# A chunked delta-rule attention in front of two gated MLPs: whole-row stages, four quarter-array matmuls at a time, and one pool of five PSUM banks

## The chip, the cores and the metric

The kernel runs on one core of a Trainium2 chip. The metric is the device time of one execution in microseconds. The core has a matmul engine (PE), which writes to eight PSUM banks, a vector engine (DVE), an activation engine (ACT), a general engine (POOL) and a queue that issues DMAs (SP). Each of them works through its own list of instructions in order, and they wait for one another with semaphores.

## The reference

Four batches of eight heads, a sequence of 768 and a head size of 48. For every head a 48 by 48 state is carried along the sequence. The result goes through two MLPs over 3072 tokens.

```python
k_n = k / (np.linalg.norm(k, axis=-1, keepdims=True) + 1e-06)
for t in range(S):
    kt, vt, bt = (k_n[:, :, t], v[:, :, t], beta[:, :, t, None])
    y[:, :, t] = np.einsum('bhd,bhde->bhe', q[:, :, t], state)
    v_old = np.einsum('bhde,bhd->bhe', state, kt)
    state = state + bt[:, :, :, None] * np.einsum('bhd,bhe->bhde', kt, vt - v_old)
...
rms = np.sqrt(np.mean(x * x, axis=-1, keepdims=True) + 1e-06)
xn = x / rms * rms_g
g = xn @ w_gate
silu = g * (1.0 / (1.0 + np.exp(-g)))
x = silu * (xn @ w_val) @ w_out
...
h = x @ w_in
sp = np.where(h > 20.0, h, np.log1p(np.exp(np.minimum(h, 20.0))))
y = (h * np.tanh(sp)) @ w_out
```

## The kernel before

The sequence is cut into twelve rows of 64 steps. A row holds 32 heads: 16 pairs, a pair's two heads in the two halves of the 128 partitions. Within a row the recurrence becomes matmuls, and for that a triangular 64 by 64 system is inverted per head. One inversion serves a segment of two rows and runs mostly on DVE (`inlane`): it begins with `comp` (L488) and ends with the transposes into `X` and `yc` (L580, L584). Two small PE stages for each row then finish it (`merge32`, L601 and L611). The inversion of segment s+1 is worked on while the rows of segment s run.

A row `r` is a list of stages (`chain_row`). Its stages are, with the line of their main instruction:

- `turn_q`, `turn_k` (L480): transposes of q and k on PE; `norm`, `scale_k` (L407, L420, L430, L431): the norms of a later row's k; `products` and `scores` (`gram`, L465, L472): k times k for a later segment, k times q for this row. DVE takes both out of PSUM with a mask (L472, tile `A` or `PT`).
- `residual` (L778): state times k, subtracted from v by DVE (L784).
- `values` (L799): the inverse times that, copied by ACT into `ve` (L801).
- `outputs` (L817 for the state's part, L825 for the row's own): the result `po`, copied out by ACT (L832), scaled by DVE (`scale_x`, L873) and transposed for the MLP (`to_x`, L888).
- `kv_update` (L854): adds k times values to the state `sx` on DVE (L862).

Four of these stages are done in two halves (`r0 r1`, `v0 v1`, `o0 o1`, `k0 k1`), two batches in a half. The state `sx` is spread: a pair's two 48 by 48 states stand as a block diagonal over 128 partitions and 96 columns, so that one matmul of 128 rows and 96 columns serves two heads. Row 0 has no state to read and row 11 none to write.

Beside a row run the first third of the first MLP (`part_a`: `pg`, `pv`, `pd`, L201 to L203 and L218 to L220), the inversion, and at some rows the splitting of weights into a high and a low part (`convs`, L122 to L159). `merge` interleaves these streams by planned costs (`C`), so that each engine gets one fixed list. Row orders are written out by hand: `EVEN`, `ODD`, and `R0`, `R1` for the first two rows. After row 11 come the rest of the weights, the rest of the first MLP and the second one, all of it matmuls of 128 by 128.

The attention has five PSUM banks: two in `ps_c` for the four halved stages, three in `ps_p` for the rest.

Of the kernel before, what the change touches and what calls it, by code (L numbers as in the profile page):

```python
# [21 lines left out]
    EVEN="nA q0 r1 x1 q1 r0 p v0 o0 k0 v1 s0 o1 k1 nB s1 x0".split(),  # L22
    ODD="q0 nA r0 r1 q1 nB c0 x1 v0 v1 p o0 c1 s0 o1 k0 d0 g x0 d1 k1 h s1".split(),
    R0="x1 r1 r0 q0 q1 p nA v0 v1 o0 o1 s0 nB k0 s1 x0 k1".split(),
    R1="r0 nA q0 x1 q1 c0 p r1 v0 o0 c1 nB v1 o1 s1 g s0 d0 k0 d1 k1 x0 h".split(),
    PRE="n2 t00 t01 w1 g0 s1 w2 s2 n3 t10 | t11 c g1 c c s3 t20 c t21 | t30 g2 t31 w3 g3".split(),
    C=dict(n=0.263, q=0.454, r=0.262, p=1.6, v=1.308, o=1.237, k=1.065, s=0.184, x=0.323, c=0.14, d=0.231, g=2.2, h=1.6),
# [30 lines left out]
def kernel(  # L58
# [14 lines left out]
    nc = tc.nc  # L73
# [193 lines left out]
    def phase_b1():  # L267
# [14 lines left out]
        ps_c = st_a.enter_context(pool("ps_c", 2, space=PSUM))  # L282
        ps_p = st_a.enter_context(pool("ps_p", 4 - P["PSD"], space=PSUM))
# [25 lines left out]
        sx = [kp.tile([128, 2, 2, 2, 2, D], F32, name=f"sx{i}") for i in range(2)]  # L309

        kT_t, A_t, X11_t, v_t, x_t, nr_t = {}, {}, {}, {}, {}, {}

# [15 lines left out]
        def load_v(r):  # L328
            if r < NR:
                v_t[r] = rp.tile([128, 16, D], F32, tag="v", name="v")  # L330
                load(v_t[r], v, r)
# [4 lines left out]
        def setup():  # L336
            qsrc = beta[:, :, 0:2 * C].rearrange("b (j e) (r f h t) -> e f r (b j) h t", e=2, r=2, f=2, t=16)
            def load_bq(r):
                for g in range(4):
                    nc.sync.dma_start(out=bq[g * 32:g * 32 + 32, r], in_=qsrc[g // 2, g % 2, r])  # L340
# [20 lines left out]
            for t in vep + sx:  # L361
                nc.gpsimd.memset(t, 0.0)
# [28 lines left out]
            for e in range(2):  # L391
                for f in range(2):
                    for r in range(2):
                        p0 = e * 64 + f * 32 + r * 16
                        nc.sync.dma_start(out=bl[p0:p0 + 16], in_=bsrc[e, f, r])
# [41 lines left out]
        def turn_k(r, bp, ps=None):  # L437
# [5 lines left out]
            if r > 3:  # L443
                need(("p", r - 4), ("r", r - 4, 0), ("r", r - 4, 1))
# [3 lines left out]
        def products(r, soft=False):  # L448
# [3 lines left out]
            if rl == 0:  # L452
                need(*([("v", r - 3, 0), ("v", r - 3, 1)] if sg > 1 else []))
                A_t[sg] = As[sg % 2]
            need(("T", r, 0), ("T", r, 1))
            gram(("G", r), kT_t[r], kT_t[r], mneg, A_t[sg][:, rl * 16:rl * 16 + 16, :], soft)
            yield 1

        def gram(key, kT, xT, mask, dst, soft=False):

            pss = [ps_p.tile([128, 8, 64], F32, tag="pp", name="pp") for _ in range(2)]
            for i in range(8):
                for j, e in ((0, 0), (1, 1), (0, 1), (1, 0)):
                    rows, sl = slice(j * 64, (j + 1) * 64), slice(e * 64, (e + 1) * 64)
                    nc.tensor.matmul(pss[j][sl, i, :], kT[rows, i // 2, i % 2, sl], xT[rows, i // 2, i % 2, sl])  # L465
# [9 lines left out]
        def turn(nat, bp, dstT, key, ps=None):  # L475
            if ps is None:
                ps = ps_p.tile([128, 4, 128], F32, tag="pp", name="pp")
# [115 lines left out]
        def merge32(r, X11, Z):  # L593
# [3 lines left out]
            ps = ps_p.tile([128, 16, 32], F32, tag="pp", name="pp")  # L597
# [9 lines left out]
            ps = ps_p.tile([128, 16, 32], F32, tag="pp", name="pp")  # L607
# [99 lines left out]
        def quick_products(r):  # L707
# [4 lines left out]
            def small(lhsT, rhs, groups=(0, 32, 64, 96), ps=None):  # L712
                if ps is None:
                    ps = ps_p.tile([128, 16, 32], F32, tag="pp", name="pp")
# [39 lines left out]
        def chain_row(r):  # L754
# [14 lines left out]
            def residual(bp):  # L769
                done.add(("r", r, bp))  # L770
                if r == 0:
                    return
                need(("s", r, bp))
                ps = ps_c.tile([128, 8, D], F32, tag="c", name="c")
                for b in range(2):
                    for jj in range(2):
                        for e in range(2):
                            nc.tensor.matmul(  # L778
                                ps[e * 64:(e + 1) * 64, b * 4 + jj * 2:b * 4 + jj * 2 + 2, :],
                                kT[:, bp * 2 + b, jj, e * 64:(e + 1) * 64],  # L780
                                sx[bp][:, b, jj, e],
                            )
                R = vv[:, bp * 8:bp * 8 + 8, :]
                nc.vector.tensor_tensor(out=R, in0=R, in1=ps, op=ALU.subtract)  # L784
# [7 lines left out]
            def values(bp):  # L792
                ps = ps_c.tile([128, 8, D], F32, tag="c", name="c")
                need(("r", r, bp), ("Y", r))
                for i in range(8):
                    u = bp * 8 + i
                    for e in range(2):
                        o = e * 64
                        nc.tensor.matmul(ps[o:o + 64, i, :], Y[o:o + 64, rl * 16 + u, :], vv[o:o + 64, u, :])  # L799
                for e in range(2):  # L800
                    nc.scalar.copy(vep[bp][e * 64:(e + 1) * 64, :, e, :], ps[e * 64:(e + 1) * 64])  # L801
                if bp == 1:
                    need(("v", r, 0))
                done.add(("v", r, bp))
                if bp == 1:
                    load_v(r + 1)
                yield 1

            def outputs(bp):
                need(("v", r, bp), ("p", r), ("s", r, bp) if r else ("p", r))  # L810
                ps = ps_c.tile([128, 2, 2, 2, D], F32, tag="c", name="o")
                halves2 = [slice(b * 64, (b + 1) * 64) for b in range(2)]
                if r > 0:
# [428 lines left out]
```

## Time and profile before

| | us |
|---|---|
| median of 3 runs | 1229.4 (1228.05 to 1229.65) |
| the profiled execution | 1227.23 |
| span in its profile | 1225.3 |
| PE busy | 1132.1 (92%) |
| DVE busy | 751.1 (61%) |
| ACT busy | 507.6 (41%) |
| POOL busy | 536.5 (44%) |

Shares of the whole span say little here, because the attention stands only in the first 490 us or so. Times in the rows below are microseconds from the start of the span. A row of a timeline gives start, duration, engine, line, operation, tiles and shapes, the number of instructions it merges, and in brackets how long the engine was idle before it and what it waited for. A matmul in 32-bit floats leaves two records, so a stage of 32 matmuls shows as x64.

### The profile page before, as it was taken

How to read it: one execution, taken by the hardware profiler on the slowest of the kernel's cores; microseconds unless marked ns; L12 is line 12 of the kernel's file. 1: busy time of each engine (PE TensorE's matmuls, PEld its weight loads, DVE VectorE, ACT ScalarE, POOL GpSimd, SP SyncE). 2: the span in 40 equal slices, each digit the busy share in tenths (PEclk: the TensorE clock that was granted, in tenths of full speed). 3: DMA queues.
4: the chain of work that ended last, by engine and by line, in shares of the span. 5: the costliest groups of instructions: out<-in, count | busy, mean ns of one | idle time of the engine just before them, and what ended most of it. 6: DMA issues, size and time to landing. Idle time of an engine off the chain costs nothing.

```text
span 1225.3 us, 30099 instructions
## 1 busy us (share of the span) xinstructions
PE 1132.1 (92%) x13044; PEld 1093.0 (89%) x13044; DVE 751.1 (61%) x1155; ACT 507.6 (41%) x878; POOL 536.5 (44%) x442
## 2 busy tenths in 40 slices
PE   6675889899898987999999999988999999999998
PEld 6664779788797877999999999988999999999998
DVE  7999995869688699455555542368434433343333
ACT  3344435353434554212111111163757555555672
POOL 7466584747636365334434432244323232232232
PEclk9668989899899998999999999998999999999999
DMA  6133231323222645434333231421111101111101
GB/s 151 30 80 92 67 79 55 79 54 79 54 66 66 182 143 168 129 112 147 112 109 102 84 113 65 142 91 58 33 40 40 39 14 40 39 40 40 36 5 26
DMA packets 121044, 95.05 MB, mean 78 GB/s; under 512 B 80336, under 2 KB 103504, under 8 KB 120912
## 3 DMA queue, kind: packets, MB, share of 16 engines
q1 hardware_dynamic: 108816, 69.53, 20.4%
q10 hardware_dynamic: 12096, 23.60, 5.7%
q8 instruction: 102, 1.67, 0.6%
q14 instruction: 30, 0.25, 0.1%
HBM read 64.80 MB, written 28.31 MB: 76 GB/s over the span
## 4 chain that ended last, share of the span: by engine, by line
PE 64%; DVE 12%; issue 2%; POOL 1%; ACT 1%; DMA 0%; SPq 0%; POOLq 0%; DVEq 0%
PE pd L1138 5%; PE pd L1139 5%; PE pd L1137 5%; PE ph L202 5%; PE ph L201 5%; PE ph L203 5%; PE pv L201 3%; PE pd L218 3%; PE pd L219 3%; PE pd L220 3%; PE pv L202 3%; PE pv L203 3%; PE pg L201 3%; PE pg L203 3%; PE pg L202 3%; DVE t L142 2%
## 5 line engine op out<-in xcount | busy, mean ns | idle before, releaser
L1185 POOL TENSOR_TENSOR gl<-t,gh 128x512 fp32r<-128x512 f32 x96 | 125.2, 1305 | 254.6 <-DVE gh L1184 253.2
L246 POOL TENSOR_TENSOR hl<-sg,hh 128x512 fp32r<-128x512 f32 x72 | 106.6, 1481 | 172.7 <-DVE hh L245 165.0
L201 PE MATMUL ph<-xh,wih 128*128 128x256 f32 x576 | 162.8, 283 | 4.6 <-DVE t L1181 4.6
L202 PE MATMUL ph<-xl,wih 128*128 128x256 f32 x576 | 162.6, 282 | 0.0
L203 PE MATMUL ph<-xh,wil 128*128 128x256 f32 x576 | 162.5, 282 | 0.0
L236 ACT ACTIVATE sg<-pg 128x512 f32<-128x512 f32 x72 | 43.0, 597 | 229.5 <-PE pg L203 202.2
L218 PE MATMUL pd<-hh,woh 128*128 128x256 f32 x432 | 125.7, 291 | 11.1 <-ACT par L937 6.4
L1137 PE MATMUL pd<-wqh,gh 128*128 128x384 f32 x384 | 130.3, 339 | 1.9 <-DVE wqh L158 1.9
L1138 PE MATMUL pd<-wql,gh 128*128 128x384 f32 x384 | 130.3, 339 | 1.7 <-POOL wql L159 1.7
L1139 PE MATMUL pd<-wqh,gl 128*128 128x384 f32 x384 | 130.0, 338 | 0.0
L201 PE MATMUL pv<-xh,wvh 128*128 128x256 f32 x432 | 127.3, 295 | 0.0
L201 PE MATMUL pg<-xh,wgh 128*128 128x256 f32 x432 | 126.2, 292 | 0.0
L202 PE MATMUL pg<-xl,wgh 128*128 128x256 f32 x432 | 122.6, 284 | 3.9 <-POOL xl L894 3.6
L220 PE MATMUL pd<-hh,wol 128*128 128x256 f32 x432 | 122.3, 283 | 4.1 <-POOL wol L159 4.1
L219 PE MATMUL pd<-hl,woh 128*128 128x256 f32 x432 | 122.5, 284 | 1.0 <-POOL hl L246 1.0
L202 PE MATMUL pv<-xl,wvh 128*128 128x256 f32 x432 | 123.3, 285 | 0.0
L203 PE MATMUL pv<-xh,wvl 128*128 128x256 f32 x432 | 123.2, 285 | 0.0
L203 PE MATMUL pg<-xh,wgl 128*128 128x256 f32 x432 | 122.3, 283 | 0.0
L1181 DVE TENSOR_TENSOR t<-t,ph 128x512 f32<-128x512 f32 x96 | 65.2, 680 | 83.4 <-ACT t L1179 83.4
L242 DVE TENSOR_TENSOR sg<-sg,pv 128x512 f32<-128x512 f32 x72 | 49.4, 686 | 107.0 <-PE pv L203 104.2
L201 PEld LDWEIGHTS ph<-xh,wih 128*128 128x128 f32 x576 | 109.8, 191 | 4.8 <-DVE t L1181 4.8
L202 PEld LDWEIGHTS ph<-xl,wih 128*128 128x128 f32 x576 | 109.9, 191 | 0.0
(197 smaller groups left out, 3007.8 us busy)
## 6 DMA issues: line engine op xcount, KB each, us to landing
raw<-in_moe_w_out_dram SPq DMA_DIRECT2D x28, 384.0 KB, 3.7
raw<-in_moe_w_in_dram SPq DMA_DIRECT2D x16, 384.0 KB, 3.8
kh<-in_k_dram SPq DMA_DIRECT2D x24, 192.0 KB, 3.6
qp<-in_q_dram SPq DMA_DIRECT2D x24, 192.0 KB, 4.3
v<-in_v_dram SPq DMA_DIRECT2D x24, 192.0 KB, 3.9
raw<-in_moe_w_gate_dram SPq DMA_DIRECT2D x12, 384.0 KB, 4.0
raw<-in_moe_w_val_dram SPq DMA_DIRECT2D x12, 384.0 KB, 3.6
xh_d<-xh SPq DMA_DIRECT2D x12, 384.0 KB, 3.2
```

The lines of the kernel that those rows point to most:

```text
L201: nc.tensor.matmul(ps[:, f, :], wh[:, kt, sl], xh[:, kt, :], start=(kt == 0), stop=False)
L202: nc.tensor.matmul(ps[:, f, :], wh[:, kt, sl], xl[:, kt, :], start=False, stop=False)
L203: nc.tensor.matmul(ps[:, f, :], wl[:, kt, sl], xh[:, kt, :], start=False, stop=(kt == KD - 1))
L218: nc.tensor.matmul(ps, wh[:, f, sl], hh[:, f, :], start=(i + f == 0), stop=False)
L219: nc.tensor.matmul(ps, wh[:, f, sl], hl[:, f, :], start=False, stop=False)
L220: nc.tensor.matmul(ps, wl[:, f, sl], hh[:, f, :], start=False, stop=last)
L246: nc.gpsimd.tensor_tensor(out=hl, in0=sg, in1=hh.bitcast(F32), op=ALU.subtract)
L1137: nc.tensor.matmul(ps, gh[:, f, sl], wh[:, f, :], start=(m + f == 0), stop=False)
L1138: nc.tensor.matmul(ps, gh[:, f, sl], wl[:, f, :], start=False, stop=False)
L1139: nc.tensor.matmul(ps, gl[:, f, sl], wh[:, f, :], start=False, stop=last)
L1181: nc.vector.tensor_tensor(out=t, in0=t, in1=ps, op=ALU.mult)
L1185: nc.gpsimd.tensor_tensor(out=gl, in0=t, in1=gh.bitcast(F32), op=ALU.subtract)
```

## The change

`residual`, `values` and `kv_update` become one stage for the whole row, and the state's part of `outputs` becomes a stage of its own for the whole row (`of_state`, in the row lists `y`). The state is no longer spread: `sx` is one tile, and each head's 48 by 48 state is read by a matmul of 64 rows, 64 columns of weights and 48 streamed columns. These matmuls are issued so that four in a row lie in the four quarters of the array, and they write two banks. For that the two halves of the partitions are swapped for two of the batches, and so v, beta and the k products of those batches are laid out swapped; v is loaded by four DMAs in place of two, and beta by 16 and 16 in place of 8 and 8. `kv_update` stands ahead of the outputs, DVE adds the state in two instructions of 128 partitions in place of four of 48, and ACT copies `po` in two pieces. All five banks are in one pool. The row lists, `PRE` and the planned costs are new.

```diff
-    EVEN="nA q0 r1 x1 q1 r0 p v0 o0 k0 v1 s0 o1 k1 nB s1 x0".split(),
-    ODD="q0 nA r0 r1 q1 nB c0 x1 v0 v1 p o0 c1 s0 o1 k0 d0 g x0 d1 k1 h s1".split(),
+    EVEN="r nA q0 x1 q1 y p v k o0 nB o1 s0 s1 x0".split(),
+    ODD="r nA q0 q1 x1 y nB c0 p v c1 k o0 d0 o1 g s0 x0 d1 h s1".split(),
...
-    C=dict(n=0.263, q=0.454, r=0.262, p=1.6, v=1.308, o=1.237, k=1.065, s=0.184, x=0.323, c=0.14, d=0.231, g=2.2, h=1.6),
+    C=dict(n=0.263, q=0.454, r=0.8, y=0.8, p=1.6, v=1.6, o=1.0, k=1.2, s=0.184, x=0.323, c=0.3, d=0.3, g=1.6, h=1.6),
...
-        ps_c = st_a.enter_context(pool("ps_c", 2, space=PSUM))
-        ps_p = st_a.enter_context(pool("ps_p", 4 - P["PSD"], space=PSUM))
+        ps_a = st_a.enter_context(pool("ps_a", 6 - P["PSD"], space=PSUM))
...
             def load_bq(r):
                 for g in range(4):
-                    nc.sync.dma_start(out=bq[g * 32:g * 32 + 32, r], in_=qsrc[g // 2, g % 2, r])
+                    for bp in range(2):
+                        o = g * 32 + bp * 16
+                        nc.sync.dma_start(
+                            out=bq[o:o + 16, r], in_=qsrc[(g // 2) ^ bp, g % 2, r, bp * 8:bp * 8 + 8]
+                        )
...
+            def residual():
+                done.add(("r", r))
+                if r == 0:
+                    return
+                need(("s", r))
+                pss = [bank(8, D) for _ in range(2)]
+                for i, (b, jj) in enumerate(units()):
+                    for j, e in ((0, 0), (1, 1), (0, 1), (1, 0)):
+                        nc.tensor.matmul(
+                            pss[j][part(e ^ (b // 2)), i, :], kT[part(j), b, jj, part(e)], sx[part(j), b, jj, e]
+                        )
+                for j, ps in enumerate(pss):
+                    R = vv.rearrange("p (i j) d -> p j i d", j=2)[:, j]
+                    nc.vector.tensor_tensor(out=R, in0=R, in1=ps, op=ALU.subtract)
...
+            def values():
+                need(("r", r), ("Y", r))
+                pss = [bank(8, D) for _ in range(2)]
                 for i in range(8):
+                    for bp, o in ((0, 0), (1, 1), (0, 1), (1, 0)):
+                        u = bp * 8 + i
+                        nc.tensor.matmul(
+                            pss[bp][part(o ^ bp), i, :], Y[part(o), rl * 16 + u, :], vv[part(o), u, :]
+                        )
...
-                for j2 in range(2):
-                    o = j2 * 64
-                    d = sx[bp][o:o + D, :, :, :, j2, :].rearrange("p b j e d -> p (b j e) d")
...
+                for e, ps in enumerate(pss):
+                    d = sx[:, :, :, e, :].rearrange("p b j d -> p (b j) d")
+                    nc.vector.tensor_tensor(out=d, in0=d, in1=ps, op=ALU.add)
```

The first place is DVE's list at the turn from an odd row to an even one, where a new inversion begins. Before:

```order
L862 TENSOR_TENSOR sx_188<-sx_188,kv 48x8x48 x2
L472 TENSOR_TENSOR A_182<-pp,mneg 128x8x64 x2
L873 SCALAR_TENSOR_TENSOR po<-po,rv,gB 128x384
L407 TENSOR_REDUCE ss<-sq 128x16
L488 SCALAR_TENSOR_TENSOR comp<-A_182,h_165 128x1024
L784 TENSOR_TENSOR v<-v,c 128x384
L495 STREAM_TRANSPOSE N__170<-comp 128x1024
L784 TENSOR_TENSOR v<-v,c 128x384
```

With the change:

```order
L487 TENSOR_TENSOR A_179<-pp,mneg 128x8x64 x2
L893 SCALAR_TENSOR_TENSOR po<-po,rv,gB 128x384
L487 TENSOR_TENSOR A_179<-pp,mneg 128x8x64 x2
L893 SCALAR_TENSOR_TENSOR po<-po,rv,gB 128x384
L800 TENSOR_TENSOR v<-v,pp 128x8x48 x2
L503 SCALAR_TENSOR_TENSOR comp<-A_179,h_162 128x1024
L420 TENSOR_REDUCE ss<-sq 128x16
L510 STREAM_TRANSPOSE N__167<-comp 128x1024
```

The even row's two subtractions (`v`) now stand ahead of `comp` and the norm's sum (`ss`) behind it; the state's addition (`sx`) of the odd row has gone up, to behind `yc`.

The second place is DVE's list in the middle of an odd row, from the sum `ss` to the scores `PT`. Before:

```order
L407 TENSOR_REDUCE ss<-sq 128x16
L784 TENSOR_TENSOR v<-v,c 128x384
L570 TENSOR_REDUCE X__171<-pr 128x4x16
L784 TENSOR_TENSOR v<-v,c 128x384
L430 RECIPROCAL rn<-nr 128x16
```

With the change:

```order
L800 TENSOR_TENSOR v<-v,pp 128x8x48 x2
L529 TENSOR_TENSOR pr<-X__168,T_4664 128x1024
L420 TENSOR_REDUCE ss<-sq 128x16
L585 TENSOR_REDUCE X__168<-pr 128x4x16
L529 TENSOR_TENSOR pr<-X__168,T_4664 128x768
L585 TENSOR_REDUCE X__168<-pr 128x4x16
L443 RECIPROCAL rn<-nr 128x16
L588 TENSOR_REDUCE X__168<-prp 128x4x16
L487 TENSOR_TENSOR PT<-pp,mpos 128x8x64 x2
```

The reciprocal `rn`, which needs two POOL instructions on `ss`, now stands behind two sums and a product in place of one sum and two subtractions.

The third place is PE's list in the same odd row, without the rows of `part_a` between. Before:

```order
L799 MATMUL c<-v,A_183 64x48 x16
...
L465 MATMUL pp<-QT,kT_181 64x64 x32
...
L817 MATMUL o<-sx_188,QT 64x2x48 x8
L825 MATMUL o<-ve_186,PT 64x96 x8
...
L854 MATMUL kv<-ve_185,kh_175 48x96 x8
...
L480 MATMUL pp<-ident,kh_174 128x128 x4
L465 MATMUL pp<-kT_180 64x64 x32
L601 MATMUL pp<-X_4637,A_182 32x32 x32
```

With the change:

```order
L813 MATMUL pp<-sx,QT 64x48 x32
...
L478 MATMUL pp<-QT,kT_178 64x64 x32
...
L832 MATMUL pp<-v,A_180 64x48 x32
...
L881 MATMUL pp<-ve_182,kh_172 64x48 x16
L881 MATMUL pp<-ve_183,kh_172 64x48 x16
...
L848 MATMUL pp<-ve_183,PT 64x96 x8
L616 MATMUL pp<-X_4977,A_179 32x32 x32
L478 MATMUL pp<-kT_177 64x64 x32
```

The values (L832) now come behind the scores (L478), and the k products that stood ahead of the first `merge32` matmuls (L601, now L616) come behind them. When the values begin, the state's products hold two of the five banks and the scores two more.

## Rows read from the trace of the kernel before

**Rows 1.** Windows: PE, loads, DVE, ACT, POOL busy (counts), PE clock, DMA share, GB/s.

```profile
60.00:134.00 74.00, 53.10 (x1282) 46.53 (x1280) 72.31 (x105) 36.59 (x72) 43.01 (x34) 0.77 0.31 77
134.00:206.00 72.00, 63.77 (x1159) 57.80 (x1158) 55.98 (x79) 29.42 (x61) 44.96 (x31) 0.95 0.27 68
...
275.40:341.10 65.70, 58.99 (x1075) 53.53 (x1075) 52.58 (x74) 25.82 (x54) 41.43 (x29) 0.95 0.24 62
...
403.50:487.00 83.50, 69.81 (x884) 64.85 (x878) 76.01 (x122) 42.88 (x98) 44.36 (x42) 0.96 0.58 181
```

**Rows 2.** Timeline of DVE through one segment (rows 6 and 7).

```profile
274.50 0.95 DVE L407 TENSOR_REDUCE ss<-sq 128x16 f32<-128x768 f32 x1 [3.01 <-ACT sq L405]
275.37 1.27 DVE L488 SCALAR_TENSOR_TENSOR comp<-A,h 128x1024 f32<-128x1024 f32 x1
...
290.62 1.11 DVE L862 TENSOR_TENSOR sx<-sx,kv 48x384 f32<-48x384 f32 x2
...
310.24 1.21 DVE L570 TENSOR_REDUCE X__171<-pr 128x64 f32<-128x1024 f32 x1
...
314.20 0.25 DVE L430 RECIPROCAL rn<-nr 128x16 f32<-128x16 f32 x1 [2.28 <-POOL nr L421]
314.37 1.36 DVE L514 TENSOR_TENSOR pr<-X__171,T 128x768 f32<-128x768 f32 x1
...
319.97 1.28 DVE L472 TENSOR_TENSOR PT<-pp,mpos 128x512 f32<-128x512 f32 x2
...
323.26 1.92 DVE L584 STREAM_TRANSPOSE yc<-N__170 128x1024 f32<-128x1024 f32 x1
...
344.56 0.56 DVE L784 TENSOR_TENSOR v<-v,c 128x384 f32<-128x384 f32 x1 [2.21 <-PE c L778]
```

**Rows 3.** What DVE waited for from 134 to 403 us: total, times, longest.

```profile
DVE rn L430 <- POOL nr L421: 6.9, 3, 2.3
```

**Rows 4.** Timeline of PE through the same segment: its waits and the `merge32` stages.

```profile
271.19 1.20 PE L611 MATMUL pp<-A,N__170 32*32 32x32 f32 x64
...
299.33 0.55 PE L888 MATMUL pp<-ident,po 128*128 128x128 f32 x3 [1.86 <-DVE po L873]
...
310.38 1.95 PE L799 MATMUL c<-v,A 64*64 64x48 f32 x32 [3.44 <-DVE v L784]
...
327.65 0.28 PE L201 MATMUL pv<-xh,wvh 128*128 128x256 f32 x1
327.77 0.28 PE L202 MATMUL pv<-xl,wvh 128*128 128x256 f32 x1
...
329.98 1.20 PE L601 MATMUL pp<-X,A 32*32 32x32 f32 x64
...
340.85 1.20 PE L611 MATMUL pp<-A,N__170 32*32 32x32 f32 x64
```

**Rows 5.** Timeline of PE in row 4, at full clock: the halved stages and the scores.

```profile
204.56 0.88 PE L778 MATMUL c<-sx,kT 128*64 128x96 f32 x16
...
208.18 1.16 PE L465 MATMUL pp<-QT,kT 64*64 64x64 f32 x64
...
211.58 1.14 PE L799 MATMUL c<-v,A 64*64 64x48 f32 x32
...
213.91 0.88 PE L817 MATMUL o<-sx,QT 128*64 128x96 f32 x16
...
216.63 0.87 PE L854 MATMUL kv<-ve,kh 128*48 128x96 f32 x16
```

**Rows 6.** The start: beta's DMAs on SP, their landing (KB, us), and DVE.

```profile
8.05 2.58 SPq L340 DMA_DIRECT2D qc<-in_beta_dram  x4
...
12.06 3.23 SPq L340 DMA_DIRECT2D qc<-in_beta_dram  x4
...
qc<-in_beta_dram SPq DMA_DIRECT2D x8, 2.0 KB, 2.8
...
18.39 2.01 DVE L626 TENSOR_SCALAR qc<-qc 128x32 f32<-128x32 f32 x2
```

More of the change, by code (lines that the diff above doesn't have):

```diff
@@ L308, in phase_b1, with part @@
         vep = [kp.tile([128, 8, 2, D], F32, name=f"ve{i}") for i in range(2)]
-        sx = [kp.tile([128, 2, 2, 2, 2, D], F32, name=f"sx{i}") for i in range(2)]
+        sx = kp.tile([128, B, 2, 2, D], F32, name="sx")
         kT_t, A_t, X11_t, v_t, x_t, nr_t = {}, {}, {}, {}, {}, {}
+        def part(i):
+            return slice(i * 64, (i + 1) * 64)
         def src(a, r, e):
@@ L330, in load_v @@
                 v_t[r] = rp.tile([128, 16, D], F32, tag="v", name="v")
-                load(v_t[r], v, r)
+                for e in range(2):
+                    for bp in range(2):
+                        us = slice(bp * 8, bp * 8 + 8)
+                        nc.sync.dma_start(out=v_t[r][part(e ^ bp), us], in_=src(v, r, e)[:, us])
         def flat(t):
@@ L393, in setup @@
                     for r in range(2):
-                        p0 = e * 64 + f * 32 + r * 16
-                        nc.sync.dma_start(out=bl[p0:p0 + 16], in_=bsrc[e, f, r])
+                        for bp in range(2):
+                            p0 = (e ^ bp) * 64 + f * 32 + r * 16 + bp * 8
+                            nc.sync.dma_start(out=bl[p0:p0 + 8], in_=bsrc[e, f, r, bp * 8:bp * 8 + 8])
             load_k(4)
@@ L767, in turn_q, with units, of_state @@
                 yield 1
-            def residual(bp):
-                done.add(("r", r, bp))
+            def units():
+                return [(b, jj) for b in range(B) for jj in range(2)]
+            def residual():
+                done.add(("r", r))
                 if r == 0:
                     return
[L773 to L784, printed above, removed]
+                need(("s", r))
[8 more added lines that the diff above has]
+                    nc.vector.tensor_tensor(out=R, in0=R, in1=ps, op=ALU.subtract)
+                yield 1
+            pos = []
+            def of_state():
+                if r == 0:
+                    return
+                need(("s", r), ("Q", r, 0), ("Q", r, 1))
+                pos.extend(bank(2, 2, 2, D) for _ in range(2))
+                for i in range(8):
+                    bp, jj, e = i // 4, (i // 2) % 2, i % 2
+                    for j, b in ((0, 0), (1, 1), (0, 1), (1, 0)):
+                        nc.tensor.matmul(
+                            pos[j][part(b), bp, jj, e, :],
+                            QT[part(j), bp * 2 + b, jj, part(e)], sx[part(j), bp * 2 + b, jj, e],
+                            start=(i == 0), stop=False, skip_group_check=True,
+                        )
+                done.add(("y", r))
                 yield 1
@@ L918, in chain_row @@
             if r:
-                need(*[(c, r - 1, i) for c in "ov" for i in range(2)])
+                need(("v", r - 1), ("o", r - 1, 0), ("o", r - 1, 1))
             for name in order(r):
```

119 lines of the change are left out of this document (51 added, 68 removed).

## The prediction

> **What bounds the kernel now.** I read the windows first, cut where each inversion begins. While two rows run, PE is busy 63.77 of 72.00 us and 58.99 of 65.70, and DVE 55.98 and 52.58 [rows 1]. No engine is full, so the segment is a chain that passes from engine to engine. In the first segment (60 to 134 us) DVE is full with 72.31 of 74.00, and after the last inversion it is busy 76.01 of 83.50 [rows 1]; in these two stretches only DVE's own work counts.
>
> DVE's timeline shows where the chain runs. The inversion is one section: `comp` begins at 275.37 and `yc` ends at 323.26 + 1.92 = 325.18 [rows 2], which is 49.8 us in which DVE idles little but for one wait of 2.28 us, `rn` for POOL's `nr` [rows 2]. This wait comes three times between 134 and 403 us, 6.9 us together [rows 3]. From `yc` to the end of the last `merge32` (340.85 + 1.20 = 342.05 [rows 4]) come 16.9 us in which PE sets the pace, since `merge32` stands behind other matmuls in its list. From the end of the earlier `merge32` (271.19 + 1.20 = 272.39 [rows 4]) to `comp` there are 3.0 us, and there DVE waits 3.01 us in front of `ss` for ACT [rows 2]. So a segment is 49.8 of DVE, 16.9 of PE, and some 3 of turn: 69.7 us. PE's waits inside the DVE section, such as 3.44 us for `v` [rows 4], are slack, not bound.
>
> **What PE saves, and where it goes.** At full clock a half stage of 16 records costs 0.88 (`residual`, state's outputs), 0.87 (`kv_update`) and 1.14 for `values` [rows 5], so a row pays 2 x (0.88 + 0.88 + 0.87 + 1.14) = 7.54 us. After the change each is 64 records of 64 rows and 48 columns. The nearest row is the scores: 64 records, 64 columns, 1.16 us [rows 5]. Four of these are 4.64. So PE saves 2.9 us a row; with ten full rows, 1.7 in row 0 and 2.3 in row 11 that is 33 us, the most that this part can give; the least is nothing or a loss, if 48 columns in quarters have a higher price per record than 64 in the same shape. I take 1.16 for the work, and ask whether it reaches the end. Inside the DVE section it doesn't: PE there only waits longer. In even rows `to_x` waits for `po`, 1.86 us now [rows 4], and will wait several. In odd rows the state's products hold two of five banks, the transposes one and the scores two, so that `values` waits until DVE takes the scores out (`PT`, 319.97 [rows 2]), 5 us before `yc` ends.
>
> On this price the Trainium skill speaks against the change: its page "TensorE: Matmul & The Clock Gate", section "Wait — 56ns, not 53.3ns?", says that matmuls never start closer than about 25 ns, however few columns they have. By it 64 records would be 1.6 us, a stage would gain little over two halves, and the sum would be some 4 us higher, an estimate. The row disagrees: 64 records in 1.16 us are 18 ns each [rows 5].
>
> **The DVE section.** Two subtractions of 0.56 [rows 2] move ahead of `comp`: -1.1. The state's addition goes from four instructions to two; a pair took 1.11 [rows 2], so -1.1. The sum `ss` moves in behind `comp`: +0.95 [rows 2]. The wait for `nr` shrinks: between `ss` and `rn` stood two subtractions and a sum (0.56 + 1.21 + 0.56, about 2.3), and now two sums and a product (1.21 + 0.95 + 1.36, about 3.5; prices in [rows 2], 0.95 being that of a 768-column sum as of `ss`), so -1.2 of 2.28. Together -2.5 for each of three segments. Bounds: 0, if PE's later `products` keep DVE waiting, to -3.7, if the wait goes whole.
>
> **The turn.** `comp` now stands behind `residual` and both subtractions. From the end of `merge32` that is 1.2 + 1.1 and some 0.3 of passing on, 2.6 against 3.0: -0.4, three times. In the fourth segment it is other: `comp` began at 341.1 [rows 1], 1.0 before that `merge32` ended, and now it comes 2.6 behind it: +3.6. In return the subtractions no longer wait in the section (2.21 us [rows 2], and a second of about 0.3) and are gone from it: -1.1 - 1.1 - 2.5 + 3.6 = -1.1.
>
> **From `yc` to `merge32`.** Today the first `merge32` of the segment starts at 329.98 [rows 4], 4.8 us after `yc`. Now `values` starts with the first half of `PT` (about 320.8). Behind it stand 36 matmuls of `part_a` at 0.12 (327.65 to 327.77 [rows 4]): 4.3; `values` 1.1, `kv_update` 1.1, the outputs' own part about 1.7, two transposes about 1.0, and about 0.8 of waiting for ACT's copies. That is 10.0 us, so that `merge32` starts at 2.6 after `yc`, not 4.8. From there on it is given back: the k products, which stood ahead, come behind with the transposes of k and a wait for their copy, about 2 us. I take 16.5 for 16.9 and count it as 0; bounds -3 and +1.
>
> **Start, first segment and tail.** Beta comes by more DMAs. Four issues took 2.58 us (0.65 each) and later 3.23 (0.81) [rows 6]. Sixteen issues and the two of q between them put the last one at 19.1 to 20.2, and 2.8 us from issue to landing [rows 6] gives 21.9 to 23.0. The multiplication, two instructions that took 2.01 from 18.39 on [rows 6], ended at 20.40; it need not be as slow again and will end near 22.4: +2 (bounds 1 and 3.6). Rows 0 and 1 are DVE-bound, and four additions of 0.56 fall out: -2.2. In the tail one row's two additions fall out of DVE: -1.1. PE's longer waits let its clock fall here and there: the granted clock is 0.95 [rows 1], and `values` at 310.38 took 1.95 us right after a wait of 3.44 [rows 4], against 1.14. For that +1.
>
> **Sum.** -7.5 - 1.1 - 1.2 + 2 - 2.2 - 1.1 + 1 = -10.1. On the profiled execution's 1227.23 that is 1217. The median of the runs shown, 1229.4, lies 2.2 above that execution; on its basis the forecast is **1219.5**.
>
> **Rivals.**
>
> *PE's saving comes through.* If PE is what delays the section more often than I read, or the freed PE time pulls `merge32` forward by 4 to 6 us a segment, the change gives -22 to -33 us: 1196 to 1207, I say 1201. For it: PE is busy 58.99 of 65.70, more than DVE [rows 1], and 5.8 of it a segment go. Against it: DVE's section, 49.8 of 69.7, keeps its length but for 2.5.
>
> *The banks make it slower.* `values` in odd rows is bound to DVE's `PT`. If PE stands idle there for several us, its clock falls to the lower of the two levels (1.2 of 2.4 GHz), as the 1.95 after a wait of 3.44 shows [rows 4], and the 10.0 us of work up to `merge32` run at that level until it rises: at most 10.0 x 1.95/1.14 = 17.1. `merge32` then starts at up to 320.8 + 17.1, 12.7 after `yc` and not 4.8, +7.9 a segment. It decides as soon as it costs over 2.5 us in each of four segments, which eats the 10 us. Half of the worst with 10 us of gain against it gives 4 x 4 - 10 = +6, 1236; the range of this case is 1232 to 1247. For it: five banks for two stages, the turn and the scores leave none. Against it: now PE waits in the same rows and works on `part_a` behind, and the clock was back before `merge32` (1.20 [rows 4]). The Trainium skill's page "TensorEngine Tiling (Array Packing)", section "Gotcha 1: PSUM Pressure", says that row tiles may not use one bank at the same time and must be written to different ones; a stage of the change holds two banks, which fits it, and no row of before shows the price of one that isn't free.
>
> *No change.* The DVE gain is eaten by PE's later `products` and by beta's DMAs: 1227 to 1232. For it: a segment is set by several engines in turn, so that a gain on one becomes a wait on the next.
>
> **How the numbers follow.** The forecast (1212 to 1225) has 0.52: it rests on instructions that certainly leave DVE's list. PE's saving coming through 0.12, no change 0.15, the banks 0.21. A measurement of this kernel can tell about 0.2%, 2.5 us, from no change. Faster is 0.52 + 0.12 = 0.64, same 0.15, slower 0.21. The range 1206 to 1236 leaves out most of the first rival and the half of the slower case above 1236, about 2 in 10.
>
> **What would show it.** Right: from one `comp` to the next some 67 us; the wait of `rn` for `nr` near 1 us; stages of 64 records at 1.1 to 1.2 us each; the multiplication of beta ending near 22.4; longer waits of `to_x` for `po`, and of `values` for `PT` in odd rows, without a later `merge32`. Wrong: `merge32` more than 5 us behind `yc` with matmuls of `part_a` at 0.24 ahead of it (banks and clock); `comp` to `comp` at 64 or less (PE's saving); stages of 1.6 us or more (the price of a record). A `comp` that waits long for `residual` would show that the turn, not the section, was mis-sized.

## The result: slower by 0.6%, where a gain of 0.8% was forecast

The changed kernel takes 1236.24 us (median of 4 runs, 1235.29 to 1239.0), the kernel before 1229.3 in the same comparison: a ratio of 1.0062, interval 1.0044 to 1.008. The profiled execution's span is 1234.1 us, 8.8 more than before. Where these come from is read from marks that both traces have. A segment is the time from one `comp` to the next, a section that from `comp` to the end of `yc`, and the tail what follows the last `merge32`:

| mark (us) | before | after | difference | step |
|---|---|---|---|---|
| first `comp` | 61.16 | 65.63 | +4.5 | start: +4.5 |
| `comp` of row 2 | 134.05 | 142.58 | +8.5 | first segment: +4.1 |
| `comp` of row 4 | 205.93 | 211.12 | +5.2 | -3.3 |
| `comp` of row 6 | 275.37 | 278.95 | +3.6 | -1.6 |
| end of the last `merge32` | 403.57 | 406.94 | +3.4 | -0.2 |
| last cast (`hh`, L245) ahead of full PE | 484.82 | 493.41 | +8.6 | tail: +5.2 |

So the middle gained 5.2 us, and the start, the first segment and the tail lost 13.8. Behind the last mark both traces take nearly the same, 740.5 and 740.7 us. First the windows after the change, cut as in [rows 1] and with its columns:

```profile
60.00:142.58 82.58, 56.28 (x1482) 50.77 (x1483) 74.81 (x109) 38.02 (x77) 45.29 (x37) 0.62 0.27 69
142.58:211.12 68.54, 59.82 (x1354) 55.14 (x1354) 54.16 (x74) 29.01 (x63) 40.18 (x30) 0.94 0.28 71
278.95:346.95 68.00, 58.24 (x1351) 53.68 (x1349) 51.72 (x70) 27.65 (x61) 39.10 (x29) 0.92 0.25 66
406.94:495.00 88.06, 69.12 (x1039) 64.47 (x1038) 74.28 (x120) 43.40 (x102) 42.18 (x42) 0.93 0.56 171
```

In the first segment and in the tail DVE is no longer full: 74.81 of 82.58 and 74.28 of 88.06, where it had 72.31 of 74.00 and 76.01 of 83.50 [rows 1]. The first of these windows begins 5.6 us ahead of `comp`, before only 1.2; from `comp` to `comp` it is 69.36 of 76.95 against 71.26 of 72.89. The granted clock of the first window is 0.62, where it was 0.77.

The stages of PE in row 4 at full clock, for [rows 5]:

```profile
208.97 1.15 PE L795 MATMUL pp<-sx,kT 64*64 64x48 f32 x64
214.65 1.15 PE L813 MATMUL pp<-sx,QT 64*64 64x48 f32 x64
223.48 1.15 PE L881 MATMUL pp<-ve,kh 64*64 64x48 f32 x64
```

The price of a quarter-array stage was right: 1.15 where 1.16 was taken, 18 ns for a record. The floor of about 25 ns between matmuls (the Trainium skill, "TensorE: Matmul & The Clock Gate", section "Wait — 56ns, not 53.3ns?") does not hold for these either.

DVE through rows 6 and 7, for [rows 2]:

```profile
278.95 1.28 DVE L503 SCALAR_TENSOR_TENSOR comp<-A,h 128x1024 f32<-128x1024 f32 x1
...
296.49 1.01 DVE L886 TENSOR_TENSOR sx<-sx,pp 128x384 f32<-128x384 f32 x2
...
306.60 1.82 DVE L893 SCALAR_TENSOR_TENSOR po<-po,rv,gB 128x384 f32<-128x384 f32 x1 [0.61 <-POOL rv L868]
...
311.40 1.02 DVE L800 TENSOR_TENSOR v<-v,pp 128x384 f32<-128x384 f32 x2 [1.31 <-PE pp L795]
...
319.00 0.24 DVE L443 RECIPROCAL rn<-nr 128x16 f32<-128x16 f32 x1
...
320.57 1.29 DVE L487 TENSOR_TENSOR PT<-pp,mpos 128x512 f32<-128x512 f32 x2 [0.78 <-PE pp L478]
...
326.50 1.96 DVE L599 STREAM_TRANSPOSE yc<-N__167 128x1024 f32<-128x1024 f32 x1
...
346.02 1.02 DVE L800 TENSOR_TENSOR v<-v,pp 128x384 f32<-128x384 f32 x2 [3.16 <-PE pp L795]
346.95 1.28 DVE L503 SCALAR_TENSOR_TENSOR comp<-A,h 128x1024 f32<-128x1024 f32 x1
```

The wait of `rn` for `nr` is gone, where the forecast left about 1 us of it, and three others stand in its place: 0.61 for `rv`, 1.31 for the odd row's residual, 0.78 for the scores, 2.7 together for 2.28. The section from `comp` to the end of `yc` is 49.5 us where it was 49.8. PE shows why the residual is late:

```profile
308.57 0.88 PE L908 MATMUL pp<-ident,po 128*128 128x128 f32 x3 [7.83 <-DVE po L893]
309.37 1.96 PE L795 MATMUL pp<-sx,kT 64*64 64x48 f32 x64
```

The residual stands in PE's list behind transposes that waited 7.83 us for `po`, against 1.86 [rows 4], and right after the wait it ran at the lower clock, 1.96 instead of 1.15.

### The profile page after: what moved, and what is told of

Its sections match the earlier page's. It is cut to its first block, busy times and chain, and to the rows that moved or that the text cites. A ratio compares the mean times of both kernels' runs of the same rounds, so it can differ in the third digit from the quotient of the medians.

```text
span 1234.1 us, 32286 instructions
## 1 busy us (share of the span) xinstructions
PE 1115.5 (90%) x14100; PEld 1081.8 (88%) x14100; DVE 739.8 (60%) x1133; ACT 507.9 (41%) x902; POOL 522.5 (42%) x441
## 4 chain that ended last, share of the span: by engine, by line
PE 66%; DVE 23%; POOL 4%; issue 2%; ACT 2%; SPq 2%; DMA 1%; DVEq 0%; POOLq 0%
PE pd L1158 5%; PE ph L201 5%; PE pd L1159 5%; PE ph L202 5%; PE ph L203 5%; PE pd L1157 5%; PE pd L218 4%; PE pd L219 3%; PE pd L220 3%; PE pg L201 3%; PE pg L203 3%; PE pg L202 3%; PE pv L201 3%; PE pv L203 3%; PE pv L202 3%; DVE pr L529 3%
## 5 line engine op out<-in xcount | busy, mean ns | idle before, releaser
L201 PE MATMUL pg<-xh,wgh 128*128 128x256 f32 x432 | 129.0, 299 | 0.0
L203 PE MATMUL pg<-xh,wgl 128*128 128x256 f32 x432 | 124.8, 289 | 0.0
```

What stands on the lines that cost most here:

```text
L201: nc.tensor.matmul(ps[:, f, :], wh[:, kt, sl], xh[:, kt, :], start=(kt == 0), stop=False)
L203: nc.tensor.matmul(ps[:, f, :], wl[:, kt, sl], xh[:, kt, :], start=False, stop=(kt == KD - 1))
```

## The experiments

All times are ratios to the kernel before, measured on the same chip, 95% interval behind. The changed kernel's own is 1.0062 (1.0044 to 1.008); 0.1% is 1.2 us. Each kernel has one trace, so that marks and waits are those of a single execution.

**The start.** In the kernel before, beta alone was loaded by 16 and 16 DMAs in place of 8 and 8:

```diff
-    nc.sync.dma_start(out=bq[g * 32:g * 32 + 32, r], in_=qsrc[g // 2, g % 2, r])
+    for bp in range(2):
+        o = g * 32 + bp * 16
+        nc.sync.dma_start(out=bq[o:o + 16, r], in_=qsrc[g // 2, g % 2, r, bp * 8:bp * 8 + 8])
...
```

(the second 8, `bl`, are split likewise)

> The kernel before, with beta loaded by 16 and 16 DMAs in place of 8 and 8 and nothing else changed. Theory A (at the start the changed kernel loses 3.6 us to the number of these DMAs alone, since the first inversion waits for the last of them): the multiplication of beta starts near 22.4 instead of 18.4, the first comp near 64.8 instead of 61.2, and the time rises by 3 to 4 us, about 0.3%. Rival (the shift of the start is taken up by waits later, or it came from the other parts of the change): the time stays within 1 us of the kernel before.

Measured: 1.0035 (1.0023 to 1.0047), 4.3 us slower, as theory A says. SP's issues and DVE in this kernel:

```profile
8.26 5.87 SPq L342 DMA_DIRECT2D qc<-in_beta_dram  x8
15.58 5.84 SPq L342 DMA_DIRECT2D qc<-in_beta_dram  x8
...
22.67 0.39 DVE L629 TENSOR_SCALAR qc<-qc 128x32 f32<-128x32 f32 x2 [4.01 <-DMA qc<-in_beta_dram]
65.71 1.28 DVE L491 SCALAR_TENSOR_TENSOR comp<-A,h 128x1024 f32<-128x1024 f32 x1
```

The multiplication and the first `comp` stand where the changed kernel has them (22.37 and 65.63). These DMAs alone make the start's loss. Two attempts to give part of them to ACT's queue in the changed kernel failed by their place:

> Eight of the sixteen first beta DMAs are issued from ACT's queue instead of SP's; nothing else differs, every engine's list of work is the same. Theory A (the changed kernel loses 3.6 us at the start because SP issues sixteen DMAs one behind the other, and all that follows is shifted by it): the multiplication of beta starts near 18.4 and not 22.4, the first comp near 62.0 instead of 65.6, and the time falls by 3 to 4 us to about 1232.5. Rival (the start has slack, since the first row waits for k and q anyway, or ACT's issues delay ACT's transposes as much): the first comp stays at 65 or later and the time within 1 us of the changed kernel's.

Measured: 1.0058 (1.0044 to 1.0073), the multiplication at 22.11 and the first `comp` at 66.04, as the rival says. ACT's eight issues came first of all, and SP's eight for k took 9.81 us instead of 7.17.

> Four of the last eight beta DMAs are issued by ACT in its idle time behind the first transposes (from about 12.5 us), where the earlier run with two queues put ACT's issues ahead of everything, so that k's DMAs came 2.6 us later and nothing was gained. Theory A (the start's loss is the time of SP's issues): SP issues its last beta DMA near 18.2 instead of 21.1, the multiplication starts near 20 instead of 22.4, the first comp near 63.3, and the time falls by about 2 us. Rival (issues on two queues slow each other): the multiplication stays at 22 or later and the time within 1 us.

Measured: 1.0074 (1.0062 to 1.0087). ACT's list had a copy ahead of these issues that waits until 19.7 us, so that the multiplication came at 24.74 and the first `comp` at 68.56. The intended place was first hit in the last run below.

**Row 1.** PE from the k products on, changed kernel:

```profile
118.05 1.98 PE L478 MATMUL pp<-kT 64*64 64x64 f32 x62 [2.97 <-DVE sx L886]
...
125.89 0.31 PE L626 MATMUL pp<-A,N__167 32*32 32x32 f32 x2 [1.80 <-ACT N__167 L620]
...
131.87 0.88 PE L908 MATMUL pp<-ident,po 128*128 128x128 f32 x3 [1.56 <-DVE po L893]
...
134.59 1.92 PE L616 MATMUL pp<-X,A 32*32 32x32 f32 x64
...
137.78 1.91 PE L626 MATMUL pp<-A,N__167 32*32 32x32 f32 x62 [0.29 <-ACT N__167 L620]
```

Several waits, and each stage at the lower clock (1.92 where `merge32` takes 1.20 [rows 4]). From the end of `yc` to the end of the last `merge32` it takes 19.4 us, before 14.4. DVE, which had no wait worth listing between 115 and 134 us before, now waits for the k products and for the residual of row 2:

```profile
134.72 1.29 DVE L487 TENSOR_TENSOR A<-pp,mneg 128x512 f32<-128x512 f32 x2 [1.94 <-PE pp L478]
141.64 1.02 DVE L800 TENSOR_TENSOR v<-v,pp 128x384 f32<-128x384 f32 x2 [3.79 <-PE pp L795]
```

Clock or order? The windows from 120 us on, first before, then changed:

```profile
120.00:125.00 5.00, 5.00 (x118) 4.35 (x114) 4.82 (x10) 3.79 (x7) 0.72 (x1) 0.50 0.17 65
125.00:130.00 5.00, 3.97 (x175) 3.37 (x170) 4.85 (x8) 3.33 (x7) 3.39 (x3) 0.99 0.41 82
```

```profile
120.00:125.00 5.00, 4.09 (x76) 3.73 (x73) 4.86 (x7) 3.85 (x8) 4.55 (x4) 0.50 0.27 81
125.00:130.00 5.00, 3.82 (x72) 3.52 (x72) 4.47 (x8) 3.88 (x8) 1.97 (x2) 0.50 0.00 1
130.00:135.00 5.00, 3.44 (x85) 2.72 (x85) 3.02 (x5) 1.66 (x4) 2.30 (x3) 0.50 0.01 3
```

Before, PE was busy through 120 to 125 and the clock rose to 0.99; after, PE has gaps and stays at 0.50, which is the 1.2 GHz level, until 144 us. Fillers, matmuls of the identity that nobody reads, test the clock:

```diff
-    R1="... o0 o1 s1 g s0 d0 d1 x0 h"
+    R1="... o0 o1 s1 z g s0 d0 d1 x0 h"      (z: 24 matmuls of ident by ident)
```

> 24 matmuls of the identity, which nobody reads, stand ahead of the k products of row 1, where PE waited 2.97 us for a bank; all else in the same order. Theory A (the 4.9 us lost between the end of yc and the last merge32 of row 1 are the clock: PE runs at 0.50 from 120 to 140 us, where before it was back at full clock from 125 on): with PE kept busy through the wait the granted clock from 120 to 140 is 0.9 or more, yc to the last merge32 falls from 19.4 to about 14.5 us, and the time by 4 to 5 us to about 1231.5. Rival B (the same stretch is longer because of the new order and the waits for banks and for ACT's copies): the stretch stays above 18 us, and the time within 1 us.

Measured: 1.006 (1.0047 to 1.0074), no gain; the block itself took 5.62 us, the clock was 1.00 until 125 and 0.50 from 130 on, so that theory A's condition was not reached. Then smaller blocks in all the waits (12, 8 and 3, 6):

> Matmuls of the identity that nobody reads stand in all four places where PE waits at the end of row 1: 12 ahead of the k products, 8 and 3 between the merge32 halves, 6 ahead of the result's transposes. A single block of 24 held the clock at 1.00 up to 125 us, but it took 5.6 us itself, the clock was back at 0.50 from 127 on, and the stretch from yc to the last merge32 kept its 19.4 us. Theory A (the low clock from 120 to 141 us is what this stretch lost): the clock stays at 0.9 or more from 115 to 140, the stretch falls to 16.5 us or less, the time by 3 to 4 us. Theory B (the stretch is held by the order: merge32's second half waits for ACT, which has the results' copies ahead of it, and the next merge32 stands behind the transposes that wait for DVE's scaled result): the stretch stays at 18.5 us or more whatever the clock, and the time within 1.5 us of the changed kernel.

Measured: 1.0024 (1.0014 to 1.0034), a gain of 4.7 us. Its profiled execution, though, held the clock only to 130 us, with the stretch at 18.3, and had most of its gain in the tail, which is looked at below. The same fillers with the tail's order (below) show the stretch at 16.5 and this clock:

```profile
120.00:125.00 5.00, 3.60 (x90) 3.29 (x82) 4.40 (x7) 3.27 (x8) 4.56 (x3) 0.93 0.26 69
125.00:130.00 5.00, 5.00 (x89) 4.73 (x88) 3.57 (x7) 4.18 (x8) 1.84 (x4) 0.73 0.05 16
130.00:135.00 5.00, 3.88 (x142) 3.42 (x141) 4.27 (x6) 1.88 (x5) 2.70 (x3) 1.00 0.02 3
```

The order, with no filler, `x0` behind `h` in row 1's list:

> In row 1 alone the first transposes of the result for the MLP stand at the end of the row's list, behind the second k products and both merge32 pairs, instead of ahead of them. With fillers in row 1's waits the clock was at 1.00 from 110 to 130 us, and the stretch from yc to the last merge32 was still 18.3 us of 19.4. Theory B (the order holds it: the second merge32 pair stands behind transposes that wait for DVE's scaled result until 131.8 us): the last merge32 ends 3 to 4 us earlier, at 15.5 to 16.5 us after yc, the comp of row 2 comes near 139, and the time falls by 3 to 4 us. Theory A (the low clock holds it): the stretch stays above 18 us and the time within 1 us.

Measured: the stretch is 15.6 us and the `comp` of row 2 at 139.73, as theory B says, with the clock at 0.50 until 130 and 0.84 in the 5 us behind; yet the time is 1.0054 (1.0042 to 1.0067), which its interval cannot tell from the changed kernel. In the profiled execution the gain reaches the end (a span 2.4 us shorter), but that is the fastest of its five. How much clock and order take is not sharp either: kernels with row 1 unchanged show stretches of 18.1 to 19.4, those with the smaller fillers 16.5 to 18.4, those with the new order 15.6 to 17.0.

**The tail.** DVE's waits from 404 us on, changed kernel (total, times, longest):

```profile
DVE v L800 <- PE pp L795: 9.3, 2, 8.6
DVE PT L487 <- PE pp L478: 4.9, 2, 2.6
DVE t L134 <- ACT t L129: 3.5, 1, 3.5
DVE sg L242 <- PE pv L203: 0.8, 1, 0.8
```

The first splitting instruction came at 412.59, 5.65 us after the last `merge32`, before it was 4.31; the weights landed 5.4 us after their issue and not 4.0. The first issue and ACT's first conversion, before and then changed:

```profile
403.25 1.03 SPq L122 DMA_DIRECT2D raw<-in_moe_w_gate_dram  x2
407.29 0.56 ACT L129 ACTIVATE t<-raw 128x384 f32<-128x384 f32 x1 [1.90 <-DMA raw<-in_moe_w_gate_dram]
```

```profile
406.62 1.03 SPq L122 DMA_DIRECT2D raw<-in_moe_w_gate_dram  x2
412.01 0.55 ACT L129 ACTIVATE t<-raw 128x384 f32<-128x384 f32 x1 [3.86 <-DMA raw<-in_moe_w_gate_dram]
```

Behind the first splitting instruction DVE waited 6.8 us, mostly for scores; before it was 0.75. The scores stand behind the state's products, which wait for ACT's copy of q, which stands behind ACT's conversions of those late weights. Lists of their own for rows 10 and 11:

```diff
+    E10="q0 r nA x1 q1 p y v k o0 nB o1 s0 s1 x0"
+    O11="r q0 q1 x1 p y v o0 o1 s0 x0 s1"
```

> In rows 10 and 11 alone the scores stand ahead of the state's products, and row 10's first transposes of q ahead of the residual. After the last merge32 DVE is the bound, and the changed kernel lets it wait 6.8 us there (4.9 for scores, 0.8 for a residual, 0.8 for a part of the MLP, 0.3 for the state), where before there was 0.8. Theory A (these waits come from the state's products, which stand ahead of the scores and wait for the copies of q): DVE's waits behind its first splitting instruction fall to 3 us or less, and the time by 3 to 4 us. Rival (they come from the later landing of the weights, 5.4 us from issue where it was 4.0, and would only move): the time falls by less than 1 us.

Measured: 1.0043 (1.0029 to 1.0057), 2.3 us less, which the intervals cannot tell from no gain. The waits:

```profile
DVE t L136 <- ACT t L131: 12.4, 2, 12.0
DVE sg L244 <- PE pv L205: 2.1, 1, 2.1
DVE v L802 <- DMA p_d<-par: 0.8, 1, 0.8
DVE PT L489 <- PE pp L480: 0.3, 1, 0.3
```

Scores cost 0.3 instead of 4.9. But here the weights also landed sooner, 4.3 us after their issue, so that this run alone does not separate order and landing. The other traces do in part. In six traces with the old lists of rows 10 and 11 the weights land 4.9 us or more after their issue, and the tail takes 86.4 to 88.2 us. In the fillers' run above, with the old lists too, they land after 4.0; the tail takes 82.5 and the scores cost 1.6. In six traces with the new lists it takes 83.8 to 85.3, among them 84.2 with a landing of 5.0. So an early landing and the new order each go with most of the gain, and they do not add up. Why the weights land in 4.0 us in some kernels and in 5.4 in others is open.

> Row 1's new order and the scores-first order of rows 10 and 11 together. If both losses are separate and both orders hold them: the sum of the two gains, 5 to 7 us, about 1230. If they share a cause (the tail shifts with whatever starts it): no more than the larger of the two alone.

Measured: 1.0035 (1.0023 to 1.0048), 0.08% below the tail's order alone: again no more than a hint of row 1's order.

**The middle segments.** `comp` ahead of the subtractions, which get a stage of their own (`u`); in even rows the inversion's stream also goes first into `merge`:

```diff
-    EVEN="r nA q0 x1 q1 y p v k ..."
+    EVEN="r q0 u nA x1 q1 y p v k ..."      (e8: nA behind q1; e12: nA behind p)
```

> In even rows from row 2 on comp stands ahead of the two subtractions of the residual, which come behind the transpose after it; PE's stages are in the same order but for what lies between them. Theory A (the segment is one chain of DVE's section and merge32, and the changed kernel's comp starts 4.1 us later than its operand allows, since it stands behind the subtractions, which wait for the residual): each of four segments is shorter by some 3 us (4.1 less the 1.0 of the subtractions that now lie inside), the time falls by 9 to 12 us to about 1226. Rival B (PE's stages bound the segment, so that DVE waits for them later): the waits of DVE for scores and results grow by as much, and the time falls by less than 3 us.

Measured: 1.0086 (1.0072 to 1.0101). The last three segments are 71.2, 68.3 and 68.3 us for 68.5, 67.8 and 68.0; `ss` waited 7.9 us in all for ACT's squares and the scores cost 6.1.

> As the run with comp ahead of the subtractions, and the norm's squares and sum moved further back, behind both transposes of q. There the sum waited 2.3 us for ACT's squares, and the first transpose 0.9 us for merge32, which still reads its target, so that of 4.1 us nothing was left. Theory A (comp's position is worth what these two waits leave: the first transpose of N begins 0.1 us behind merge32 and not 4.2, less the subtractions and the sum that now lie behind it): each of the four segments from row 2 on is 2 us shorter, and the time falls by 6 to 9 us to about 1229. Rival (another wait takes its place inside the section, for the residual of the odd row or for the scores): the segments keep 67.8 us within 0.7, and the time falls by less than 3 us.

Measured: 1.0053 (1.0041 to 1.0065), not told from the changed kernel, the last two segments at 67.7 and 66.9. `comp` and its transpose came early, and the sum waited:

```profile
208.03 1.28 DVE L503 SCALAR_TENSOR_TENSOR comp<-A,h 128x1024 f32<-128x1024 f32 x1
210.22 2.04 DVE L510 STREAM_TRANSPOSE N__167<-comp 128x1024 f32<-128x1024 f32 x1 [0.92 <-PE pp L626]
...
216.66 0.95 DVE L420 TENSOR_REDUCE ss<-sq 128x16 f32<-128x768 f32 x1 [2.36 <-ACT sq L418]
```

> As the run of both orders, and comp ahead of the subtractions in even rows with the norm's squares behind the scores, so that the sum no longer waits for them right behind comp (2.4 to 4.2 us there, three times, which ate the gain of the early transpose). Theory A (the section from comp is DVE's own work, so that each us of wait taken out of it shortens the segment): 2 to 3 us less in each of four segments from row 2 on, and a time 6 to 9 us below the run of both orders, about 1222. Rival (PE's stages take its place: scores, residual of the odd rows): less than 2 us below it.

Measured: 1.0102 (1.0088 to 1.0116). Row 10's list had no `u`, so this run leaves out the subtraction in row 10. Its sections grew to 56 us, with waits of 12.9 for POOL's product and 12.8 for the scores. Theory A of these three runs fell: each wait taken out of the section uncovered the next.

The transposes that make PE wait, behind the odd row's residual:

> The first transposes of an even row's result for the MLP are issued behind the odd row's residual instead of ahead of it. Theory A (PE's wait of up to 7.8 us for the scaled result holds back the odd row's residual, which stands behind it, and DVE then waits 1.3 us for that in its section): the waits of the transposes fall from 26.7 us in all to under 10, DVE's wait in the subtraction of the odd rows goes, and the time falls by 3 to 6 us. Rival B (the odd row waits for the scores' banks anyway, so that PE only waits elsewhere): the sections from comp to yc keep 49.4 and 49.5 us and the time stays within 1.5 us.

Measured: 1.0142 (1.0125 to 1.016). The waits for `po` fell from 26.7 to 12.6 us, and PE waited 16.5 us for `xl`, which is made from these transposes; the wait of `rn` for `nr` was back with 6.5 in all.

The outputs ahead of `kv_update`, in even rows:

```diff
-    EVEN="... p v k o0 nB o1 s0 s1 x0"
+    EVEN="... p v o0 o1 s0 k s1 nB x0"
```

> In even rows from row 2 on the outputs and their scaling stand ahead of kv_update again, which is the one part of the new row order undone. Theory A (the scaled result comes 2 to 9 us later than before, since the outputs stand behind kv_update; PE's transposes wait for it 26.7 us in all, the odd row's residual stands behind them, and DVE waits 1.3 us for that and 0.6 for rv in its section): the waits of the transposes fall below 16 us, DVE's wait for the odd row's residual goes, the segments from rows 4 and 6 fall from 67.9 to about 66 us, and the time by 3 to 6 us, to about 1231. Rival (the section's waits only change their name): the segments keep 67.9 within 0.7 us and the time falls by less than 1.5.

Measured: 1.0048 (1.0035 to 1.0062), 1.7 us less, short of the 3 to 6 expected and within the intervals. The odd row's wait for its residual went, and `rn` waited again:

```profile
DVE v L800 <- PE pp L795: 9.5, 3, 3.2
DVE sg L242 <- PE pv L203: 7.3, 3, 2.8
DVE rn L443 <- POOL nr L434: 6.5, 3, 2.2
```

The sections fell to 48.6 us and `merge32` came 1.3 later behind `yc`, so that the segments kept 68.4: the rival. PE's `values` waited 14.9 us in all for `PT`, where it was 0.9.

Does PE's work count in these segments at all? The state's products twice:

> The changed kernel, with the state's products of rows 2 to 9 issued twice, which adds 32 matmuls of 64 rows and 48 columns to PE in eight rows, 8 x 1.1 = 8.7 us of PE at full clock, and nothing to any other engine. Theory A (PE's work inside DVE's sections is not on the path, so that neither saving nor adding it moves the end): the time rises by less than 2 us, and PE's waits for the scaled result, 26.7 us between 142 and 407, shrink by about as much as was added in even rows. Rival (PE's work counts whole, and the saving was lost elsewhere): the time rises by 7 to 9 us, 0.6 to 0.7%.

Measured: 1.0094 (1.008 to 1.0108), 3.9 us for 8.7 us of added work, between both theories; with the intervals of both kernels it is anything from 1 to 7. From the `comp` of row 2 to the last `merge32` the trace has 3.5 us more. PE's waits for `po` did not shrink as theory A wants (26.2 us for 26.7). So a part of PE's work counts at this place, ahead of the scores that DVE waits for, near half by the medians.

**Together.**

> The late ACT issues of beta, row 1's fillers and the scores-first order of rows 10 and 11 together. If the losses are three separate ones: the gains add, about 2 + 4.5 + 2.5 = 9 us, 1227, at the level of the kernel before or just below. If row 1's fillers and the tail's order had the same gain (the fillers' profiled execution had most of its gain in rows 10 and 11): about 5 to 6 us, 1230.5.

Measured: 1.0034 (1.0021 to 1.0046), with the start worse than in the changed kernel (multiplication at 25.38).

> The same with the outputs ahead of kv_update in even rows. If the order of outputs and kv_update is worth 3 to 6 us by itself, this run is that much below the one without it, about 1222 to 1224, and faster than the kernel before. If that order is worth nothing: the same time as without it, within 1.5 us.

Measured: 1.005 (1.0037 to 1.0062): the outputs' order gains nothing here.

> Fillers in row 1's waits and the scores-first order of rows 10 and 11, the start as in the changed kernel. Theory A (separate losses): ratio to the kernel before near 1.0005, that is the fillers' 4.7 us and the tail's 2.4 us together, about 1229. Rival (they share the gain, since most of the fillers' gain was seen in rows 10 and 11): ratio 1.002 to 1.003, as with the fillers alone, about 1231.

Measured: 1.0018 (1.0008 to 1.0028). Theory A's 1.0005 lies outside this interval and the rival's 1.002 inside. That speaks for the rival: on top of the fillers (1.0024 alone) the tail's order gives nothing that the intervals can tell, which fits the tails above.

> Fillers in row 1's waits, the scores-first order of rows 10 and 11, and four of beta's last eight DMAs issued by ACT from about 12.4 us on. Theory A (three separate losses): the multiplication starts near 20.5 instead of 22.4 and the time is 1.5 to 2 us below that of the run without this, 1226 to 1227.5, no slower than the kernel before. Rival (two queues slow each other): the multiplication stays near 22.4 or later, and the time is that of the run without it or more.

Measured: 0.9992 (0.9984 to 1.0001), no difference to the kernel before.

```profile
15.66 2.90 SPq L358 DMA_DIRECT2D qc<-in_beta_dram  x4
...
19.80 1.02 DVE L652 TENSOR_SCALAR qc<-qc 128x32 f32<-128x32 f32 x2 [1.08 <-DMA qc<-in_beta_dram]
62.64 1.28 DVE L512 SCALAR_TENSOR_TENSOR comp<-A,h 128x1024 f32<-128x1024 f32 x1
```

With the multiplication at 19.80 and not 22.56, and `comp` 3.4 us earlier, the time is 0.26% lower than without that, 3.2 us, and the intervals do not meet. The three repairs are 0.7% together, as much as the change had cost. They do not take the losses away whole: against the kernel before, this trace still has +1.5 us at the start, +0.7 in the first segment and +3.1 in the tail, and the middle's -5.4 pays for these.

## Why the prediction was wrong

**The step that failed** is "in these two stretches only DVE's own work counts". From the busy shares before, -2.2 was taken for the first segment and -1.1 for the tail; they measured +4.1 and +5.2. These two make two thirds of the distance between -10.1 and +8.8. DVE was full there because what it waited for came in time. After the change it waited 3.8 and 1.9 us at the end of row 1 (for the residual and the k products) and 6.8 in the tail, there in part because the weights landed later. The share told what DVE did, not that nothing could become later than it. Fillers and the tail's order, which give DVE no work less, took 0.44% off the time (the run of both, 1.0018).

**The start** was forecast to be +2 and is +4.5. The multiplication was right (22.37 to 22.76, forecast near 22.4). What was missed lies between the end of the multiplication and the first `comp`, 42.9 us where it was 40.8, which the prediction had left as it was. Of these 2.1 us, 1.4 come in the first instructions, up to the next `rn`: 16.7 us for 15.3. Small ones that otherwise take 0.2 to 0.4 us took 1.0 to 1.5 there in four places, before in two. The kernel before with the split DMAs shows 16.6, so that this too came with the DMAs; why is not shown.

**The middle.** From the `comp` of row 2 to the last `merge32` the forecast was -9.4 (of its three turns of -0.4 one lies ahead of that `comp`), the trace has -5.2. Right were the price of a stage, the way of the wait for `nr`, the turn (2.08 us behind `merge32`, forecast 2.6), `comp` later in the fourth segment (+3.0, forecast +3.6), and `merge32` sooner behind `yc` but no earlier in its end (16.4 for 16.9). The sections were to lose 2.5 each and lost 2.0, 0.2 and 0.3, the fourth 2.3 of 4.7; the three new waits of rows 6 and 7, 2.7 us, are what the sum left out there. "PE there only waits longer" was too short: the odd row's residual is in the same list behind that wait, and DVE waits for the residual.

Two sums of the prediction do not come out of their own terms. That `merge32` starts 2.6 us after `yc` does not follow: 320.8 and 10.0 is 5.6 after 325.18. The trace has 3.4, because `PT` now begins 7.9 us ahead of the end of `yc` and not 5.2; from `PT` to `merge32` it is 11.3 us for 10.0. And the banks' worst case is four times 7.9 less 10, 1251 and not 1247, half of it 1235.

**The clock** got +1 for "here and there". At the end of row 1 it stood at 0.50 from 118 to 144 us, where before it was back by 125. The kernel with fillers there is 4.7 us faster, but in its trace this stretch is only 1.1 shorter, so that what the clock alone costs is not shown.

**The rivals.** The banks' rival named 1236, but where it placed its mechanism it is not: `values` waits for `PT` and its bank 0.9 us in all between 142 and 407, and `merge32` starts 3.4 us after `yc`, not 12.7. Something like it stands once, at the end of row 1: the k products waited 2.97 us for a bank that the state's addition frees, the clock was at 0.50 behind it, and `merge32` ended 4.9 us later after `yc` than before. That PE's saving comes through was rightly held unlikely; the doubled stage shows that it is not free either.

What stays open: why the weights land later in the tail, how much of the tail's loss is this landing and how much the order, and how much of row 1's order, apart from the clock, reaches the end.

## What to carry to other kernels

Here a stretch in which one engine was 98% busy was bound by that engine only as long as the lists that feed it kept their order; with a new order, walk its inputs one by one, at the start and the end of the program above all, where no other row's work covers a wait. Count a layout's extra DMAs by SP's issue time, 0.7 us each here, when something at the start waits for the last of them. And price PE's saved work by what PE does in the time it gains: where it idled here, the next stages ran at half the clock, 1.92 us for 1.20.

## What the runs showed of the hardware

Issues on ACT's queue can slow those on SP's at the same time: eight for k took 9.81 us on SP beside eight of beta's on ACT (6.53 us), 7.17 alone. Four of beta's on ACT from 11 to 15 us cost SP next to nothing: its eight for beta took 5.95 us for 5.88 and its two for q 1.52 for 1.36. What makes the difference is not shown.
